# An expert kernel on one core: the path for an unguessed first expert is set ahead of the guessed one, each with its own transposition, and the last part copies fewer rows

## The chip, the cores and the metric

One core of one Trainium2 chip runs the kernel. The metric is the device time of one execution in microseconds; the kernel before has a median of 733.77 us over three executions (732.97 to 736.35). One more execution was profiled, and it took 737.84 us.

## What is computed

Three layers stand behind one another. The first is attention (4 batches, 8 heads, 576 positions, width 64; half the heads look at 32 neighbours, the other half at every 32nd position). The second is a dense layer, `h = x @ w_in`, `g = s * relu(h)**2 + b`, `x2 = g @ w_out`, over 2304 rows of 512. The third sends each row to one of eight experts:

```python
do_compute = x @ w_skip > 0
xc = x[do_compute]
e_idx = argmax(xc @ w_gate); gate_w = softmax(xc @ w_gate)[e_idx]
for e in range(8):
    mask = e_idx == e
    h = maximum(xc[mask] @ w1[e], 0)        # 512 -> 1024
    y[mask] = gate_w[mask, None] * (h @ w2[e])   # 1024 -> 512
out[do_compute] = xc + y                    # the other rows stay x
```

## The kernel before

The change lies in the third layer, in `experts()` (L1066 to L1173). The rows of one expert are taken in row tiles of 128, four tiles to a group. A group goes through these helpers:

- `gather` (L926): POOL issues four indirect DMAs (L930) that fetch four row tiles from `x2d` into `K["R"]` (the buffers `qkl` and `qks`).
- `turn` (L947): PE transposes each tile with four matmuls (L937), ACT rounds the result into `Xh` (L940), DVE puts the remainder into `Xl` (L944).
- `up` (L957): for each of eight slices of the hidden width 12 matmuls (L962) into one of two PSUM buffers `h`; ACT (L965) and DVE (L966) empty it.
- `down` (L971): for each row tile 24 matmuls (L975), one DVE instruction (L979) that scales and adds the kept row, and one indirect DMA on POOL (L980) that scatters the tile, 256 KB, to `out`.
- `keep_rows` (L1062): four ACT copies (L1064) that keep the gathered rows, since the next `gather` overwrites them.

The expert with the most rows is guessed before the last block of rows is routed. Its weights and its first 512 rows are loaded and its first `up` is done in the gaps of the last block (`fill`, L1072), all under `npre >= 512`, a count read into a register. This is the hot path. `down(3, ...)` (L1102) then does three of the four row tiles, a common `turn()` (L1119) transposes the next four tiles, and the If/Else at L1120 either does the fourth row tile, `down(4, ..., 3)` (hot), or loads and splits the weights of the expert and does its first group (general, L1122 to L1128). Behind it, the weights of the next expert are loaded into the raw buffers `wo0` to `wo7` by eight DMAs of SP (`load_raw`, L1130, issued in L904), and `groups` (L1143) does groups 1 to 3 and a last part `rest` of one to three row tiles. A loop over further experts (L1162) follows.

The order of the instructions on each engine is the order in the program, written out (`tc.manual_schedule()`); nothing of an If moves out of it. Engines wait for one another by counters: each engine counts its finished instructions, and the DMAs of POOL and of SP count in lanes, eight for each. A wait names a count, the same count whichever arm of an If ran. So the arm that runs must leave all counters where the other would have left them: on each engine an instruction that the source does not show waits until the engine's own work ahead of it is counted and then adds the other arm's share (an EVENT_SEMAPHORE record, or a larger step at the last instruction of the arm). POOL waits until the DMAs that are under way in each lane concerned have landed, and then adds to the lanes with one INC_SWDGE_SEM. An If without an Else has such an arm as well, for when it is skipped. An instruction behind an If that reads a tile which an arm may have written waits for the counts that this arm would have made, too.

In the executions told of here the hot path runs, one expert takes 18 row tiles (18 scatters in L980: four of the hot path, 14 behind it), so groups 1 to 3 run and a `rest` of two row tiles, and the loop of L1162 is skipped.

Of the kernel before, what the change touches and what calls it, by code (L numbers as in the profile page):

```python
# [191 lines left out]
def kernel(  # L192
# [70 lines left out]
    def c_v(n, fast=1, psum=0.0):  # L263
        return {"V": 0.06 + n / fast / 960 + psum}

    def c_a(n, psum=False):
        return {"A": (0.13 if psum else 0.16) + n / 1400}
# [4 lines left out]
    def c_dma(n):  # L272
        return {"SP": max(0.06, n / 300e3)}
# [300 lines left out]
    t = plan.add({"G": 0.3}, fill, 6, take=[fill_b])  # L574
# [13 lines left out]
    for n, (m, c) in enumerate(order):  # L588
# [35 lines left out]
        t = plan.add(c_dma(128 * 8 * 512), stage, prio - 2, take=[raw_b], lat=DMA)  # L624
        t = plan.add({"A": 0.58}, scale, prio, after=[t], take=[c_b], use=[raw_b])
        t = plan.add(c_v(512, 2), shift, prio, after=[t], use=[c_b])
        t = plan.add(c_v(512), sign, prio, after=[t], use=[c_b, raw_b])
        t = plan.add(c_v(512), low, prio, after=[t], use=[c_b, raw_b])
        t = plan.add({**c_a(512), **(c_v(512, 2) if c < HI_N else {})}, upper, prio, after=[t], take=[w_b], use=[c_b])
# [33 lines left out]
    t = plan.add({**c_a(512, True), **c_v(512)}, gate_row, 34, after=[gate_t], take=[gr_b], use=[gt_b])  # L663
# [253 lines left out]
    K = {}  # L917
# [21 lines left out]
    def turn_hi(pt, t):  # L939
        A.copy(K["Xh"][:, :, t * 128:(t + 1) * 128], pt[:])  # L940
# [5 lines left out]
    def turn():  # L946
        for t in range(4):  # L947
            if t < 3:
                pt = pm.tile([128, 4, 128], F32, name=("pt", "sx0", "sx1")[t])
            else:  # L950
                pt = ph.tile([128, 4, 128], F32, name="h")
            turn_in(pt, t)
            turn_hi(pt, t)
            turn_lo(pt, t)
# [13 lines left out]
    def down(nt, ids, rows, t0=0):  # L968
        for t in range(t0, nt):
            c = slice(t * 128, (t + 1) * 128)  # L970
            y = px.tile([128, DM], F32, name=f"x2p{K['ny'] % 3}")  # L971
            n = 0
            for f in range(NFE):
                for g, w in ((0, 0), (1, 0), (0, 1)):
                    PE.matmul(y[:], K["h"][f][:, g, c], W[NFE + f][:, w, :], start=n == 0, stop=n == 3 * NFE - 1)  # L975
                    n += 1
            yo = rp.tile([128, DM], F32, name="row")
            K["ny"] += 1
            V.scalar_tensor_tensor(yo[:], y[:], ids[:, t, 1:2].bitcast(F32), rows[t], op0=ALU.mult, op1=ALU.add)  # L979
            put = G.indirect_dma_start(  # L980
                out, bass.IndirectOffsetOnAxis(ap=ids[:, t, 0:1], axis=0),
                yo[:], None, bounds_check=NT - 1, oob_is_err=False,
            )
            tc.declare_no_dep(put.ins, group="rows", reason="the lists name each token once")
            tc.add_to_no_dep_group("rows", put.ins)
# [73 lines left out]
        V.tensor_copy(lg[:].rearrange("p t e -> p (t e)"), lt[:, 0:27])  # L1059
        rt[blk] = {"lg": lg}  # L1060

    def keep_rows():  # L1062
        for t in range(4):
            A.copy(K["E"][:, t, :], K["R"][t])  # L1064

    def experts():  # L1066
        K["h"] = [wp.tile([128, 2, 512], F32R, name=f"wo{8 + f}") for f in range(NFE)]
        K["E"] = wp.tile([128, 4, DM], F32, name="xb2")
        E = [K["E"][:, t, :] for t in range(4)]
        npre = reg(pre, slice(3, 4), NT)  # L1070

        def fill(n):  # L1072
            lo, hi = FILL[n], FILL[n + 1]
            if hi > lo:
                with tc.If(npre >= 512):
                    up(512, lo, hi)

        last_x2(fill)
        route_a(NBLK - 1)
        route_exp(NBLK - 1)  # L1080
        route_b(NBLK - 1)
        route_c(NBLK - 1)
        keep_rows()
        fill(3)
        rk, cn = (pm.tile([128, 512], F32, name=n_) for n_ in ("sx0", "sx1"))
        route_rank(NBLK - 1, rk)
        tally(cn)
        route_out(NBLK - 1)
        route_list(rt[NBLK - 1])
        lt = sp.tile([128, NL, 2], I32, name="s_")  # L1090
        gi = sp.tile([128, NL], I32, name="pts", bufs=1)
        SY.dma_start(lt[:, 0:NE * NTT, :].rearrange("p (e t) c -> p e t c", e=NE), lst[:].rearrange("(e p t) c -> p e t c", p=128, t=NTT))
        fill(4)
        finish_routing(cn)
        V.memset(gi[:], NT - 1)
        V.tensor_scalar(gi[:, 0:NE * NTT], lt[:, 0:NE * NTT, 0], NT - 1, None, op0=ALU.min)
        on = (mybir.EngineType.DVE,)
        eg = reg(meta, slice(0, 1), NE - 1, on)
        s0 = reg(meta, slice(19, 20), 4, on)
        gather(gi[:, bass.ds(eg * NTT + s0, 4)])  # L1100
        with tc.If(npre >= 512):
            down(3, K["ltp"], E)  # L1102
        def copied(e, t0, n):
            ids = sp.tile([128, 4, 2], I32, name="ids")
            V.tensor_copy(ids[:, 0:n, :], lt[:, bass.ds(t0, n), :])  # L1105
            return ids

        def group(e, g):
            ids = copied(e, e * NTT + 4 * g, 4)
            up(512, 0, 2)  # L1110
            keep_rows()
            gather(gi[:, bass.ds(e * NTT + 4 * g + 4, 4)])
            up(512, 2)
            turn()
            down(4, ids, E)

        word = reg(meta, slice(28, 29), (NE << 16) + 0xFFFF)
        e0, e1, T, ni = word & 7, (word >> 3) & 7, (word >> 6) & 31, word >> 16
        turn()  # L1119
        with tc.If(npre >= 512) as done:  # L1120
            down(4, K["ltp"], E, 3)
        with done.Else():  # L1122
            for n in range(8):
                load_raw(e0, n)
            for n in range(2 * NFE):
                split_w(n)
            with tc.If(T >= 4):
                group(e0, 0)  # L1128
        for n in range(8):
            load_raw(e1, n)  # L1130

        def rest(e, T, en, r):
            if r:
                ids = copied(e, e * NTT + (T & 28), r)
                up(max(256, 128 * r), 0, 2)
                keep_rows()
            gather(gi[:, bass.ds(en * NTT, 4)])
            G.drain()
            if r:
                up(max(256, 128 * r), 2)  # L1140
                down(r, ids, E)

        def groups(e, T, en):  # L1143
            with tc.If(T >= 8):
                group(e, 1)
                with tc.If(T >= 12):
                    group(e, 2)
                    with tc.If(T >= 16):
                        group(e, 3)
            with tc.If((T & 2) == 2) as two:  # L1150
                with tc.If((T & 1) == 1) as one_more:
                    rest(e, T, en, 3)
                with one_more.Else():
                    rest(e, T, en, 2)
            with two.Else():
                with tc.If((T & 1) == 1) as one_more:
                    rest(e, T, en, 1)
                with one_more.Else():
                    rest(e, T, en, 0)

        groups(e0, T, e1)
        with tc.If(ni > 1):  # L1162
            with tc.For_i(1, ni, 1) as i:
                turn()
                word = reg(meta, bass.ds(i + 20, 1), 0x7FF)
                e, en, T = word & 7, (word >> 3) & 7, word >> 6
                for n in range(2 * NFE):
                    split_w(n)
                for n in range(8):
                    load_raw(en, n)  # L1170
                with tc.If(T >= 4):
                    group(e, 0)
                groups(e, T, en)  # L1173
# [6 lines left out]
    for i, (blk, fc, begins, ends) in enumerate(SEQ):  # L1180
# [61 lines left out]
        t = plan.add(c_a(BLK, True), relu, i - 9000, after=[m1], take=[r_b], use=[h_b])  # L1242
        if i < SQ_A:
            t = plan.add(c_a(BLK), square_a, i - 9000, after=[t], use=[r_b])
            t = plan.add(c_v(BLK, 2), scale_g, i - 9000, after=[t, consts], use=[r_b])
        else:
            t = plan.add(c_v(BLK), square, i - 9000, after=[t, consts], use=[r_b])
        t = plan.add(c_a(BLK), g_hi_a if i < SQ_A else g_hi, i - 9000, after=[t], take=[gh_b], use=[r_b])
        t = plan.add(c_v(BLK), g_lo_a if i < SQ_A else g_lo, i - 9000, after=[t], take=[gl_b], use=[r_b, gh_b])
        gts[i] = t  # L1250
        if i < NS - 2:
            t = plan.add(c_pe(DM, 9, False), mm2, i + 1.2 - 3000, after=[t, mm2s[-1] if mm2s else None] + (w_done["o", fc] if blk < 2 else []),
                         take=xbuf if begins else [], use=[gh_b, gl_b, wbuf["o", fc]])
# [171 lines left out]
```

## Time and profile before

| what | us |
|---|---|
| median of three executions | 733.77 (732.97 to 736.35) |
| the profiled execution | 737.84 |
| its span, first to last instruction | 736.1 |
| `down(3)` of the hot path on PE | 542.98 to 559.34 |
| `turn()`, `down` of the fourth tile, branch to group 1 | 559.34 to 567.55 |
| groups 1 to 3 | 567.55 to 705.42 |
| `rest` of two row tiles | 705.42 to 728.70 |
| last scatter to the end | 729.77 to 736.1 |

Times on the profile's views are from the span's start. PE is TensorE's matmuls, PEld its weight loads, DVE VectorE, ACT ScalarE, POOL GpSimd, SP SyncE; a name with q (PEldq, POOLq, SPq) is the sequencer of that engine, which runs ahead of it and executes branches and semaphore instructions. A line of the timeline is: start, duration, engine, line, operation, output from input, count, and in brackets how long the engine had been idle and what released it.

### The profile page before, as it was taken

The page shows a single profiled execution, that of the slowest core. Times are in us where ns is not written, and L with a number is a line of the kernel's source. Part 1 is how long each engine was busy: PE and PEld are TensorE (multiplying, and loading weights), DVE is VectorE, ACT ScalarE, POOL GpSimd, SP SyncE. Part 2 cuts the span into 40 slices and gives each one's busy share as a digit, 9 for nine tenths or more (in the row PEclk, how much of TensorE's full clock was granted, in tenths as well). Part 3 has the DMA queues.
Part 4 walks back from the last instruction along what each step waited for, and adds up shares of the span by engine and source line. Part 5 has one row for each costly group of instructions (what it writes and reads, how often), then busy time and mean ns, then how long its engine had stood idle before and what let it go on. Part 6 is the DMA issues. An engine that isn't in the chain of part 4 may idle for free.

```text
span 736.1 us, 12323 instructions
## 1 busy us (share of the span) xinstructions
PE 720.6 (98%) x4481; PEld 619.7 (84%) x4486; DVE 418.7 (57%) x1173; ACT 290.3 (39%) x830; POOL 64.8 (9%) x79
## 2 busy tenths in 40 slices
PE   9989999999999999999999999999999999999995
PEld 6877889998888888888888988898787888888894
DVE  3679999945567887777756654754442222312221
ACT  4768866633344444544432223543311312203120
POOL 0000000000010001000200012010023212022131
PEclk9979999999999999999999999999999999999999
DMA  8856757602233313522031106320203701112021
GB/s 274 290 158 217 233 154 217 185 18 86 67 129 93 116 60 105 173 85 76 24 106 50 47 1 196 103 76 0 86 17 114 282 29 55 33 48 67 29 78 44
DMA packets 29742, 77.70 MB, mean 106 GB/s; under 512 B 5833, under 2 KB 6953, under 8 KB 29665
## 3 DMA queue, kind: packets, MB, share of 16 engines
q1 hardware_dynamic: 25585, 65.49, 27.9%
q0 software_dynamic: 3936, 11.03, 4.8%
q8 instruction: 41, 0.67, 0.4%
q14 instruction: 36, 0.29, 0.1%
q10 hardware_dynamic: 144, 0.22, 0.1%
HBM read 60.81 MB, written 15.91 MB: 104 GB/s over the span
## 4 chain that ended last, share of the span: by engine, by line
PE 73%; DMA 11%; DVE 7%; issue 5%; ACT 2%; POOL 1%; DVEq 0%; POOLq 0%; ACTq 0%
PE x2p L1235 21%; PE h L1192 21%; PE h L962 10%; PE x2p L975 8%; DMA lo<-wgt 7%; DVE junk L745 5%; DMA out<-row,ids 4%; PE sx L490 2%; PE pt L455 2%; PE sx L414 2%; PE sx L412 1%; PE h L1345 1%; DVE r L1200 1%; PE x2p L1027 1%; PE h L414 1%
## 5 line engine op out<-in xcount | busy, mean ns | idle before, releaser
L1192 PE MATMUL h<-xb,wi 128*128 128x384 f32 x1152 | 222.7, 343 | 0.0
L1192 PEld LDWEIGHTS h<-xb,wi 128*128 128x128 f32 x1152 | 204.8, 189 | 7.5 <-issue 0.7
L1235 PE MATMUL x2p<-wo,gh 128*128 128x512 f32 x564 | 195.0, 400 | 0.0
L1235 PEld LDWEIGHTS x2p<-wo,gh 128*128 128x128 f32 x564 | 105.9, 188 | 21.4 <-issue 0.3
L1235 PE MATMUL x2p<-wo,gl 128*128 128x512 f32 x282 | 111.0, 394 | 0.0
L962 PE MATMUL h<-xb,wi 128*128 128x512 f32 (+1 forms) x480 | 103.2, 374 | 1.4 <-DVE ids L1105 1.0
L962 PEld LDWEIGHTS h<-xb,wi 128*128 128x128 f32 x480 | 83.4, 188 | 19.4 <-issue 1.6
L975 PE MATMUL x2p<-wi,wo 128*128 128x512 f32 x432 | 99.4, 390 | 0.0
L975 PEld LDWEIGHTS x2p<-wi,wo 128*128 128x128 f32 x432 | 80.7, 188 | 16.6
L1204 ACT ACTIVATE gh<-r,sbc 128x384 fp32r<-128x384 f32 x91 | 56.1, 616 | 84.3 <-DVE r L1200 41.8
L1197 ACT ACTIVATE r<-h 128x384 f32<-128x384 f32 x96 | 47.0, 490 | 104.8 <-PE h L1192 64.1
L965 ACT ACTIVATE wo<-h 128x512 fp32r<-128x512 f32 (+1 forms) x40 | 22.2, 555 | 143.6 <-PE h L962 137.6
L1209 DVE SCALAR_TENSOR_TENSOR gl<-r,sbc,gh 128x384 fp32r<-128x384 f32 x91 | 56.1, 616 | 39.9 <-ACT gh L1204 39.1
L1200 DVE SCALAR_TENSOR_TENSOR r<-r,sbc 128x384 f32<-128x384 f32 x91 | 56.0, 616 | 37.6 <-ACT r L1197 36.1
L745 DVE SCALAR_TENSOR_TENSOR junk<-row,lo 128x512 int8<-128x512 f32 x81 | 55.8, 689 | 22.8 <-DMA lo<-wgt 21.6
L966 DVE SCALAR_TENSOR_TENSOR wo<-h,wo 128x512 fp32r<-128x512 f32 (+1 forms) x40 | 25.5, 638 | 76.0 <-ACT wo L965 74.9
L1235 PEld LDWEIGHTS x2p<-wo,gl 128*128 128x128 f32 x282 | 53.1, 188 | 8.4 <-DVE gl L1209 0.3
L864 POOL DMA_INDIRECT lst<-pay,ii x18 | 19.1, 1060 | 364.4 <-DVE ii L858 333.3
L979 DVE SCALAR_TENSOR_TENSOR row<-x2p,ids,xb 128x512 f32<-128x512 f32 x14 | 10.5, 751 | 61.7 <-PE x2p L975 61.7
L980 POOL DMA_INDIRECT out<-row,ids x14 | 13.9, 994 | 106.2 <-DVE row L979 92.8
L279 ACT CAST xb<-sx 128x192 fp32r<-128x192 f32 (+5 forms) x55 | 14.2, 299 | 18.5 <-PE sx L414 4.3
L497 DVE TENSOR_TENSOR xb<-sx,xb 128x192 fp32r<-128x192 f32 (+5 forms) x63 | 17.7, 302 | 4.2 <-ACT xb L279 3.4
(501 smaller groups left out, 774.4 us busy)
## 6 DMA issues: line engine op xcount, KB each, us to landing
wo<-in_w SPq DMA_DIRECT2D x16, 512.0 KB
lo<-wgt SPq DMA_DIRECT2D x27, 256.0 KB
wo<-in_w_out SPq DMA_DIRECT2D x12, 512.0 KB
x2d<-row SPq DMA_DIRECT2D x24, 256.0 KB
qks<-in_qkstr SPq DMA_DIRECT2D x6, 882.0 KB
wo<-in_w_in SPq DMA_DIRECT2D x10, 512.0 KB
out<-row SPq DMA_DIRECT2D x18, 256.0 KB
qkl<-in_qkloc SPq DMA_DIRECT2D x5, 864.0 KB
```

The lines of the kernel that those rows point to most:

```text
L414: PE.matmul(sc[0:nq, i * nk:(i + 1) * nk], qt, qk[0][:, k0:k0 + nk], start=not by_pe, stop=not by_pe or i == nt - 1)
L745: V.scalar_tensor_tensor(junk[:], d["rows"][t][:], 1.0, wd["w"][:], op0=ALU.mult, op1=ALU.mult, accum_out=d["lg"][:, t, x:x + 1])
L962: PE.matmul(p[:, 0:N], W[f][:, w, k * 128:(k + 1) * 128], x[:, k, 0:N], start=n == 0, stop=n == 11)
L965: A.activation(h[:, 0, 0:N], p[:, 0:N], AF.Relu)
L966: V.scalar_tensor_tensor(h[:, 1, 0:N], p[:, 0:N], 0.0, h[:, 0, 0:N].bitcast(F32), op0=ALU.max, op1=ALU.subtract)
L975: PE.matmul(y[:], K["h"][f][:, g, c], W[NFE + f][:, w, :], start=n == 0, stop=n == 3 * NFE - 1)
L1192: PE.matmul(p[:, 0:BLK], win_t[fc][:, w, k * 128:(k + 1) * 128], x[:, k, :], start=n == 0, stop=n == 11)
L1197: A.activation(d["r"][:], d["p"][:, 0:BLK], AF.Relu)
L1200: V.scalar_tensor_tensor(d["r"][:], d["r"][:], sbc[:, 0:1], d["r"][:], op0=ALU.mult, op1=ALU.mult)
L1204: A.activation(gh[:], d["r"][:], AF.Identity, bias=sbc[:, 1:2])
L1209: V.scalar_tensor_tensor(gl[:], d["r"][:], sbc[:, 1:2], gt[i][0][:].bitcast(F32), op0=ALU.add, op1=ALU.subtract)
L1235: PE.matmul(x2p[t][:], g[:, c], wout_t[fc][:, w, :], start=begins and n == 0, stop=ends and n == 2)
```

## The change

`turn()` is taken from its common place and stands once in each path. The Else arm becomes an If of its own, `npre < 512`, with the loads, the splits and the first group in it, and it stands ahead of the hot If. `keep_rows` gets a count, and `rest` copies as many row tiles as it has.

```diff
-    def keep_rows():
-        for t in range(4):
+    def keep_rows(n=4):
+        for t in range(n):
             A.copy(K["E"][:, t, :], K["R"][t])
...
-        turn()
-        with tc.If(npre >= 512) as done:
-            down(4, K["ltp"], E, 3)
-        with done.Else():
+        with tc.If(npre < 512):
+            turn()
             for n in range(8):
                 load_raw(e0, n)
             for n in range(2 * NFE):
                 split_w(n)
             with tc.If(T >= 4):
                 group(e0, 0)
+        with tc.If(npre >= 512):
+            turn()
+            down(4, K["ltp"], E, 3)
         for n in range(8):
             load_raw(e1, n)
...
                 up(max(256, 128 * r), 0, 2)
-                keep_rows()
+                keep_rows(r)
```

## Rows read from the trace of the kernel before

**Rows 1.** The page, part 1: busy time, share of the span, instructions of each engine
```profile
PE 720.6 (98%) x4481; PEld 619.7 (84%) x4486; DVE 418.7 (57%) x1173; ACT 290.3 (39%) x830; POOL 64.8 (9%) x79
```

**Rows 2.** The chain that ended last, 541 to 572 us: start, us, what
```profile
559.34 0.43 PE pt L937 x4
```

**Rows 3.** The timeline from the hot path's third tile to group 1, 547 to 570 us
```profile
559.44 0.75 DVE L979 SCALAR_TENSOR_TENSOR row<-x2p,s__5049,xb 128x512 f32<-128x512 f32 x1 [4.67 <-PE x2p L975]
...
560.46 0.97 POOL L980 DMA_INDIRECT out<-row,s__5049  x1 [3.06 <-DVE row L979]
...
560.84 5.71 PE L975 MATMUL x2p<-wi,wo 128*128 128x512 f32 x24
...
566.65 0.75 DVE L979 SCALAR_TENSOR_TENSOR row<-x2p,s__5049,xb 128x512 f32<-128x512 f32 x1 [3.73 <-issue]
...
567.55 2.95 SPq L904 DMA_DIRECT2D wo<-in_w  x4
567.55 2.81 PE L962 MATMUL h<-xb,wi 128*128 128x512 f32 x11 [0.99 <-DVE ids L1105]
567.68 0.97 POOL L980 DMA_INDIRECT out<-row,s__5049  x1 [6.24 <-DVE ids L1105]
```

**Rows 4.** Waits of SP's queue, 540 to 600 us: total, times, longest
```profile
SPq L904 <- DVE row L979: 18.0, 1, 18.0
```

**Rows 5.** Records of the If at L1120: count, ns min/median/max, first and last start
```profile
L1120 PEldq COMPARE_BRANCH  x2: 73/1862/3652, 558.7 to 562.3; - x2
...
L1120 POOLq INC_SWDGE_SEM  x1: 794/794/794, 567.8 to 567.8; - x1
```

**Rows 6.** The timeline, 726 to 737 us: the last matmuls and the last scatter
```profile
725.82 2.88 PE L975 MATMUL x2p<-wi,wo 128*128 128x512 f32 x12
...
729.77 1.00 POOL L980 DMA_INDIRECT out<-row,ids  x1 [4.42 <-DMA out<-row,ids]
```

**Rows 7.** Records of the If at L1162, which is skipped
```profile
L1162 POOLq EVENT_SEMAPHORE  x6: 17/30/695, 732.6 to 733.8; - x6
...
L1162 PEldq COMPARE_BRANCH  x1: 5046/5046/5046, 725.0 to 725.0; - x1
...
L1162 POOLq INC_SWDGE_SEM  x1: 226/226/226, 733.8 to 733.8; - x1
```

**Rows 8.** DMA queues, 560.4 to 563.2 us: packets, MB, share of 16 engines
```profile
q0 software_dynamic: 80, 0.26, 24.1%
```

**Rows 9.** Scatters of L980, whole run: time from issue to landing
```profile
DMA to landing us min/median/max: 2.7/2.8/3.8
```

**Rows 10.** DMA queues, 570 to 573.2 us
```profile
q1 hardware_dynamic: 216, 0.79, 72.4%
q0 software_dynamic: 80, 0.26, 20.2%
```

**Rows 11.** Stretches: us, busy PE, PEld, DVE, ACT, POOL, granted clock, DMA share, GB/s
```profile
60.00:62.00 2.00, 0.56 (x6) 0.43 (x5) 2.00 (x6) 1.40 (x8) 0.00 (x0) 1.00 0.58 221
...
734.00:736.00 2.00, 0.00 (x0) 0.00 (x0) 0.00 (x0) 0.00 (x0) 0.00 (x0) 0.50 0.02 4
36.00:38.00 2.00, 0.85 (x21) 0.72 (x22) 2.00 (x9) 1.66 (x9) 0.00 (x0) 0.91 0.85 331
...
46.00:48.00 2.00, 2.00 (x8) 2.00 (x7) 1.70 (x4) 0.00 (x0) 0.00 (x0) 0.53 0.06 6
```

**Rows 12.** The timeline, 606 to 660 us: the first matmuls of group 2
```profile
613.55 22.57 PE L962 MATMUL h<-xb,wi 128*128 128x512 f32 x96
```

**Rows 13.** The timeline of `rest`, 660 to 737 us: copies, emptying and matmuls
```profile
708.83 1.13 ACT L1064 COPY xb<-qkl 128x512 f32<-128x512 f32 x2
...
709.86 1.14 ACT L1064 COPY xb<-qks 128x512 f32<-128x512 f32 x2
...
711.79 6.02 PE L962 MATMUL h<-xb,wi 128*128 128x256 f32 x48 [0.46 <-DVE wo L966]
```

**Rows 14.** Records of the If at L1101, around `down(3)`
```profile
L1101 PEldq COMPARE_BRANCH  x2: 73/121/169, 539.1 to 555.1; - x2
```

## The prediction

> **What bounds the kernel now.** The page's busy times come first: PE is busy for 98% of the span [rows 1], so a change counts for what it adds to, or takes from, PE's idle time. The chain of waits then gives the place: the third tile of the hot path ends on PE at 559.34 us, where the first transposition of `turn()` starts at once [rows 2]. The timeline shows what follows: the fourth tile's 24 matmuls end at 560.84 + 5.71 = 566.55, and group 1 starts at 567.55 after 0.99 us of idleness [rows 3]. That gap is an arm's end: DVE's last instruction of the arm ends at 566.65 + 0.75 = 567.40, and SP, PE and POOL go on within 0.3 us of it. SP had waited 18.0 us for that one instruction before it loads the next expert's weights [rows 4], though no instruction of the hot arm touches the raw buffers. So instructions behind an If wait for counts that stand in for the other arm. The sequencer records of the If show POOL's part in it, an INC_SWDGE_SEM at 567.8 [rows 5]. I read next how long it takes at an If that is skipped, L1162: the last scatter is issued at 729.77 [rows 6], and POOL's INC_SWDGE_SEM comes at 733.8, behind a wait of 0.695 us, and takes 0.226 us [rows 7].
>
> **The change part by part.** The sums are made against the profiled execution (737.84 us: span 736.1 and 1.74 around it); the median of the runs is 4.07 us lower, and I carry the difference over to it.
>
> *A new wait ahead of the turn.* The general path, with a turn, a gather and four scatters in it, is now skipped just ahead of the hot turn. POOL must level its lanes there, and for that the three scatters of `down(3)` must have landed. The hot transposes read `K["R"]`, which the general path's gather writes, so PE waits for that levelling; in the kernel before nothing stood between. The steps: DVE ends the third tile at 559.44 + 0.75 = 560.19, POOL issues its scatter at 560.46 [rows 3]. Without company its 80 packets are gone by 563.2 [rows 8], 2.7 us after the issue, as in the median of the landings, 2.8 [rows 9]. But DVE's levelling at 560.2 also releases SP's eight weight loads, seven microseconds earlier than now. The row for that company stands in the trace: the fourth tile's scatter is issued at 567.68, just behind the first load at 567.55 [rows 3], and its 80 packets run only between 570 and 573.2, among 216 of the loads [rows 10]. That is up to 5.5 us; I take 5.4, since issue and loads have the same order and distance here (560.46, and about 560.3 for the load). Landing at 560.46 + 5.4 = 565.9, with 0.3 for POOL's waits and INC_SWDGE_SEM (0.226) [rows 7], PE restarts at 566.2 and not at 559.34: +6.9 us. The lower bound is 0, if PE need not wait for POOL; with a landing of 2.7 it is +4.1. Nothing covers it: behind the first transpose on PE stand the other 15, the 24 matmuls and group 1; ACT and DVE wait for the transposes, and POOL's next scatter for DVE.
>
> The Trainium skill (DMA: Bandwidth & Descriptors, section "Anatomy of one DMA — SWDGE (gpsimd) path") puts one such DMA at about 2.0 us plus its bytes over 436 GB/s, an estimate of 2.6 us for 256 KB. The 2.7 us without company agree, the 5.4 us beside the loads do not; by the page the sum below would be that of the rival with the short landing.
>
> *TensorE's clock.* After the last matmul, at 725.82 + 2.88 = 728.70 [rows 6], the granted clock is 0.50 in the stretch from 734 to 736, the lower of its two levels, 1.2 GHz [rows 11]: a silence of some 5 us lowers it. One of 1.4 us (0.56 busy of 2, at 60 to 62) does not. Mid-kernel the lower level lasted from 36 to 38 until the end of 46 to 48, some 10 us, over patchy work [rows 11]. A silence of 6.9 us should lower it too. Half speed costs half of the time that it lasts: 0 if it does not fall, 5 us if it lasts as long as there. Dense work follows here, so I take 4 us of it: +2.0.
>
> *The gap behind the fourth tile goes.* The hot arm is no longer levelled by its own last DVE instruction; group 1 needs DVE's part of the turn, done during the fourth tile. From group 1 to group 2, at such a boundary, PE's matmuls of L962 follow with no idle time in their row [rows 12]. -1.0 [rows 3], with 0 as the other bound.
>
> *`rest` copies two tiles instead of four.* The four copies hold ACT from 708.83 to 711.00, and PE waits 0.46 us for the emptying behind them [rows 13]. With two they end at 709.96, earlier by 1.04, more than the wait. -0.5; between 0 and -1.0.
>
> *Branches and code.* PE's branch over the Else took 3.652 us [rows 5], run by its sequencer ahead of matmuls in its queue. The jump over the general path now comes when the sequencer leaves `down(3)`, at 555.1 [rows 14], and ends at 558.8, still ahead of 559.34; the dearest jump, 5.046 [rows 7], would end at 560.2, inside the new wait. 0 as long as the wait is there, +0.9 if it is not. The second copy of the turn does not run, and the extra compares lie in the wait: 0. The earlier loads end before group 1's gather: 0, since PE does not wait for that gather now.
>
> The sum: +6.9 + 2.0 - 1.0 - 0.5 = +7.4. The profiled execution would take 745.2, the median 733.77 + 7.4 = 741.2 us.
>
> **The rivals.**
>
> *Short landing.* The scatter lands after 2.7 to 3.8 us [rows 9], because the loads' packets come too late to disturb it. For it: its descriptors are issued as early as the first load. Against it: the same order gave the late landing [rows 3, 10]. PE restarts at 563.5 to 564.6, +4.1 to +5.2, less 1.5, with 0 to 2 for the clock: 736.4 to 739.5, middle 737.9.
>
> *A long low clock.* As the first forecast, but the lower level lasts 10 us as at 36 to 48 [rows 11]: +5.0 instead of +2.0, 744.2. Against it: there matmuls were sparse.
>
> *PE does not wait for POOL* (the other side). The transposes need only counts of the gather ahead of the If, long landed, and PE, ACT and DVE level themselves in tenths of a microsecond. Then the two gains stay, -1.5, and at most the longest jump shows, +0.9: 732.3 to 733.2, middle 732.8, no change. It decides if the two paths' conditions are seen as exclusive, or if the reader of a tile waits only for the write that ran. Against it: SP's 18.0 us for an arm whose buffers it alone touches [rows 4]. The Trainium skill (Runtime: NRT & Kernel Launch, section "Instruction fetch mechanics") says that a branch to code not yet fetched holds its engine up. The 3.652 us of PE agree [rows 5]; by the page such a jump holds up the turn once nothing else does.
>
> **How the numbers follow.** The first case has 0.62, the long low clock 0.07, the short landing 0.14, no wait 0.17. With less or more low clock (0 to 3 us) and a landing up to half a microsecond off, the first case's own range is 738.7 to 742.7. For eight in ten the range must take in the long clock and most of the short landing: 736.8 to 744.5 leaves out the case without a wait. A measurement of this kernel can tell about 0.5%, 3.7 us, from no change. Slower than 737.4: 0.62 + 0.07 + 0.08 of the short landing = 0.77. Within: the rest of that, 0.06, and 0.15 of the case without a wait. Faster than 730.1 needs more than both gains: 0.02.
>
> **What would show it.** In the changed kernel's timeline PE's first transpose of the hot turn (L937) stands idle for some 7 us, POOL's INC_SWDGE_SEM of the skipped If comes just ahead of it and the third tile's landing ahead of that, and SP's loads are issued near 560, not 567. The granted clock falls near there. Group 1 follows the fourth tile without a gap; `rest` has two copies and no gap of 0.46. If the transposes start near 559.4, the first step is wrong; if they start near 563.5, the landing.

## The result and the profile after

The changed kernel takes 743.74 us (median of 6 runs, 740.84 to 747.30) beside 734.16 for the kernel before (6 runs): a ratio of 1.0131, 95% interval [1.0107, 1.0154], or +9.6 us where +7.4 was forecast. It was run once more beside the last experiment: 741.13 beside 733.01, ratio 1.0108 [1.0074, 1.0142], +8.1.

The timeline of the changed kernel around the hot turn (start, us, what, idle time before it and what ended it) answers to [rows 3]:

```profile
554.29 0.75 DVE L979 SCALAR_TENSOR_TENSOR row<-x2p,s__5049,xb 128x512 f32<-128x512 f32 x1 [4.67 <-PEq L1119]
555.27 5.90 SPq L904 DMA_DIRECT2D wo<-in_w  x8
555.32 0.97 POOL L980 DMA_INDIRECT out<-row,s__5049  x1 [3.05 <-DVEq L1119]
...
563.51 1.09 PE L937 MATMUL pt<-im,qkl 128*128 128x128 f32 x4 [9.32 <-DMA qkl<-x2d,gx]
...
566.81 6.99 PE L975 MATMUL x2p<-wi,wo 128*128 128x512 f32 x24
573.64 1.57 PE L962 MATMUL h<-xb,wi 128*128 128x512 f32 x6
```

PE stands idle for 9.32 us ahead of the first transposition, where it did not wait at all before [rows 2]. The four tiles' transpositions and the fourth tile's matmuls then take longer than they did, and group 1 (L962, at 573.64) follows without a gap. The releaser in brackets is named after the tile's last gather; that gather had landed long before, and what came last is POOL's levelling at the skipped If, line 1119. Its records (count, ns min/median/max, first and last start) answer to [rows 5]:

```profile
L1119 POOLq EVENT_SEMAPHORE  x5: 17/43/43, 555.8 to 562.4; - x5
L1119 PEldq COMPARE_BRANCH  x1: 3352/3352/3352, 550.6 to 550.6; - x1
...
L1119 POOLq INC_SWDGE_SEM  x1: 755/755/755, 562.5 to 562.5; - x1
```

POOL issues the third tile's scatter at 555.32, waits until 562.4 for it to land, and levels from 562.5 to 563.25; PE goes on 0.26 us later. PE's jump over the general path (3.35 us from 550.6) ends at 554.0, hidden. The scatter shares its time with the loads; the DMA queues from its issue to 562.2 answer to [rows 10]:

```profile
q1 hardware_dynamic: 412, 1.54, 67.5%
q0 software_dynamic: 80, 0.26, 9.4%
```

75 of its 80 packets (q0) run before 560, and the last of them between 561.5 and 562. SP's waits, which answer to [rows 4], show that the loads are let go earlier:

```profile
SPq L904 <- DVEq L1119: 10.7, 1, 10.7
```

In stretches of 2 us: the busy times of PE, PEld, DVE, ACT and POOL, and then the granted clock (third figure from the end), the DMA share and GB/s; as [rows 11]:

```profile
556.00:558.00 2.00, 0.00 (x0) 0.00 (x0) 0.00 (x0) 0.00 (x0) 0.29 (x1) 1.00 0.69 162
558.00:560.00 2.00, 0.00 (x0) 0.00 (x0) 0.00 (x0) 0.00 (x0) 0.00 (x0) 0.82 0.86 307
560.00:562.00 2.00, 0.00 (x0) 0.00 (x0) 0.00 (x0) 0.00 (x0) 0.00 (x0) 0.50 1.00 391
...
566.00:568.00 2.00, 2.00 (x9) 1.81 (x8) 1.53 (x3) 1.29 (x3) 0.00 (x0) 0.50 1.03 416
568.00:570.00 2.00, 2.00 (x8) 1.53 (x7) 0.55 (x1) 0.00 (x0) 0.00 (x0) 0.62 0.39 160
570.00:572.00 2.00, 2.00 (x10) 1.67 (x9) 0.00 (x0) 0.00 (x0) 0.00 (x0) 1.00 0.02 8
```

It falls to 0.50 (the lower level, 1.2 GHz) during PE's silence and is back at 1.00 only during the fourth tile: the 0.62 from 568 to 570 puts that near 569.5, an estimate, so PE works at the lower level for some 6.0 us. Last, the timeline of `rest`, as [rows 13]:

```profile
711.44 11.72 PE L962 MATMUL h<-xb,wi 128*128 128x256 f32 x96
...
714.85 1.13 ACT L1064 COPY xb<-qkl 128x512 f32<-128x512 f32 x2
...
723.00 11.07 PE L975 MATMUL x2p<-wi,wo 128*128 128x512 f32 x48
```

The line of the kernel before that answers to the last of these:

```profile
717.64 11.05 PE L975 MATMUL x2p<-wi,wo 128*128 128x512 f32 x48
```

Two copies, no wait on PE: from 711.44 to 723.00 are 11.56 us, where the same part took 717.64 - 705.42 = 12.22 before.

To keep the account I measure from the start of DVE's scaling of the third tile (L979) to the start of the first transposition (A), and from there to group 1's first matmul (B). In the timeline of the kernel before the first transposition is this line (the chain of [rows 2] counts it from the end of the matmul ahead of it, 559.34):

```profile
559.18 0.60 PE L937 MATMUL pt<-im,qkl 128*128 128x128 f32 x4
```

Before: A = -0.26 (559.18 against 559.44), B = 8.37 (to 567.55), in it the gap. After: A = 9.22, B = 10.13. Later runs show B without gap and at the full clock as 7.21. So the change costs 9.48 in A, 2.92 for the clock in B, and gives 1.16 (the gap) and 0.66 (`rest`) back: +10.6 us.

The two profiled spans differ by only 741.0 - 736.1 = 4.9 us, because the execution profiled before had a stretch at the lower clock from 36 to 48 us [rows 11] that this one lacks; the third tile's scaling comes at 554.29 here and at 559.44 there. Of the fourteen profiles five have such a stretch (before, e2_hot_first, e4_seven_dmas, e6_busy_pe, e9_busy30). The spread of the times goes with the clock, too: of the 24 executions of the kernel before that stand beside e7_late_put, the six above 736 us have a mean granted clock of 0.990 or 0.991, the others (731.5 to 733.8) 0.993 to 0.999. This is why what follows reads the trace in place beside the medians.

### The profile page after: what moved, and what is told of

Its sections match the earlier page's. It is cut to its first block, busy times and chain, and to the rows that moved or that the text cites. A ratio compares the mean times of both kernels' runs of the same rounds, so it can differ in the third digit from the quotient of the medians.

```text
span 741.0 us, 12346 instructions
## 1 busy us (share of the span) xinstructions
PE 718.6 (97%) x4485; PEld 618.6 (83%) x4486; DVE 418.6 (56%) x1173; ACT 290.1 (39%) x828; POOL 64.7 (9%) x79
## 4 chain that ended last, share of the span: by engine, by line
PE 86%; DMA 6%; issue 4%; ACT 1%; DVE 1%; POOL 1%; DVEq 0%; POOLq 0%; ACTq 0%
PE h L1193 28%; PE x2p L1236 27%; PE h L962 10%; PE x2p L975 7%; DMA out<-row,ids 4%; DMA qkl<-x2d,gx 3%; PE sx L490 2%; PE pt L455 2%; PE sx L412 2%; PE sx L414 2%; PE h L1346 1%; PE x2p L1027 1%; PE sx L483 1%; PE h L414 1%; PE pt L937 1%
## 5 line engine op out<-in xcount | busy, mean ns | idle before, releaser
L962 PE MATMUL h<-xb,wi 128*128 128x512 f32 (+1 forms) x480 | 103.0, 373 | 0.0
L962 PEld LDWEIGHTS h<-xb,wi 128*128 128x128 f32 x480 | 83.5, 188 | 17.5 <-issue 0.2
L979 DVE SCALAR_TENSOR_TENSOR row<-x2p,ids,xb 128x512 f32<-128x512 f32 x14 | 10.5, 751 | 61.8 <-PE x2p L975 61.8
L980 POOL DMA_INDIRECT out<-row,ids x14 | 13.9, 995 | 105.8 <-DVE row L979 92.5
```

The lines of the kernel that those rows point to most:

```text
L962: PE.matmul(p[:, 0:N], W[f][:, w, k * 128:(k + 1) * 128], x[:, k, 0:N], start=n == 0, stop=n == 11)
```

## The experiments

All were timed beside the kernel before on the same chip, and the ratio is to that; the series were run on several chips. A and B as above, us; the column of the scatter's issue to INC_SWDGE_SEM is filled where the skipped path stands ahead of the hot turn or of the fourth tile:

| run | A | B | A + B | scatter's issue to INC_SWDGE_SEM | median | before | ratio |
|---|---|---|---|---|---|---|---|
| before | -0.26 | 8.37 | 8.11 | | | | |
| changed | 9.22 | 10.13 | 19.35 | 7.2 | 743.74 | 734.16 | 1.0131 [1.0107, 1.0154] |
| e1_rest_only | -0.25 | 8.36 | 8.11 | | 732.73 | 733.72 | 0.9998 [0.9976, 1.0019] |
| e2_hot_first | -0.25 | 8.37 | 8.12 | | 733.75 | 733.72 | 1.0002 [0.9982, 1.0023] |
| e3_no_gather | 0.94 | 7.25 | 8.19 | 0.8 | 734.29 | 733.72 | 1.0009 [0.9986, 1.0031] |
| e4_seven_dmas | 2.84 | 8.87 | 11.71 | 0.9 | 735.62 | 733.72 | 1.0019 [0.9999, 1.0039] |
| e5_no_loads | 5.26 | 9.51 | 14.77 | 3.3 | 739.32 | 733.33 | 1.0079 [1.0049, 1.0109] |
| e6_busy_pe | 9.79 | 7.20 | 16.99 | 5.6 | 743.98 | 733.33 | 1.0127 [1.0093, 1.0161] |
| e7_late_put | -0.26 | 8.41 | 8.15 | | 732.01 | 733.33 | 0.9990 [0.9966, 1.0015] |
| e8_shared_turn | -0.26 | 9.50 | 9.24 | 3.1 | 734.67 | 733.33 | 1.0018 [0.9993, 1.0042] |
| e9_busy30 | 8.22 | 7.21 | 15.43 | 5.6 | 743.70 | 735.41 | 1.0102 [1.0071, 1.0133] |
| e10_skip_pe | -0.26 | 8.37 | 8.11 | | 735.05 | 735.41 | 0.9990 [0.9968, 1.0012] |
| e11_after_again | 7.39 | 8.90 | 16.29 | 5.4 | 741.13 | 733.01 | 1.0108 [1.0074, 1.0142] |
| e12_busy30_again | 8.06 | 7.22 | 15.28 | 5.5 | 740.71 | 733.01 | 1.0093 [1.0066, 1.0120] |

My theory: the hot turn waits for POOL, because a skipped path that gathers into the row tiles stands ahead of it, and POOL waits there for the third tile's scatter; the loads make that scatter late, and the silence lowers the clock. The main rival: PE is held by the jump over the longer general path.

**The small part alone.** The kernel before with `keep_rows(r)` in `rest`.

> The kernel before with one part of the change alone: rest copies only the row tiles that are left. Theory: the emptying of PSUM behind the copies comes earlier and PE's 0.46 us of waiting goes, so 0.4 to 0.7 us less than the kernel before. Rival: the time won is given back further on in the last part, no difference at all.

In the trace `rest` takes 11.52 us (700.46 to 711.98) and not 12.22, as in the changed kernel. In time 0.7 us of 733 is below what the runs can tell.

**The order.** The two Ifs change places:

```diff
+        with tc.If(npre >= 512):
+            turn()
+            down(4, K["ltp"], E, 3)
         with tc.If(npre < 512):
             turn()
...
-        with tc.If(npre >= 512):
-            turn()
-            down(4, K["ltp"], E, 3)
```

> The changed kernel with its two Ifs in the other order: the hot path with its turn first, the general path (skipped) behind it. Theory (the hot turn waits because a skipped path that gathers into the row tiles stands ahead of it): the 9.3 us of idleness on PE go, the clock does not fall, and group 1 waits about 1 us for the last levelling on DVE as in the kernel before: 733 to 734.5 us. Rival (the general path now holds a turn more, and it is the jump over it that holds PE up): 3 to 5 us stay, 737 to 739.

The whole loss is gone. Its timeline:

```profile
556.00 0.60 PE L937 MATMUL pt<-im,qkl 128*128 128x128 f32 x4
...
557.66 5.71 PE L975 MATMUL x2p<-wi,wo 128*128 128x512 f32 x24
564.37 10.98 PE L962 MATMUL h<-xb,wi 128*128 128x512 f32 x46 [0.99 <-DVEq L1122]
```

The turn starts at once, and the gap of 0.99 is back ahead of group 1. The general path with its own turn is there as in the changed kernel, so its length is not what costs; its place is.

**The gather.** The changed kernel, and the general path's first group leaves out its gather; that path does not run with these inputs.

```diff
-        def group(e, g):
+        def group(e, g, ga=True):
...
-            gather(gi[:, bass.ds(e * NTT + 4 * g + 4, 4)])
+            if ga:
+                gather(gi[:, bass.ds(e * NTT + 4 * g + 4, 4)])
...
-                group(e0, 0)
+                group(e0, 0, ga=False)
```

> The changed kernel; the general path's first group leaves out its gather (that path is skipped with these inputs). Order, turns, branches and scatters stay. Theory (PE waits for POOL's levelling only because the skipped path writes the row tiles by a gather): the transposes start within 1 us of the third tile's end, the clock stays, 732 to 734 us. Rival (any skipped path with DMAs of POOL in it, or the branch itself, holds PE up): 741 to 744 as the changed kernel.

```profile
555.85 0.63 PE L937 MATMUL pt<-im,qkl 128*128 128x128 f32 x4 [1.03 <-DVEq L1120]
```
```profile
L1120 PEldq COMPARE_BRANCH  x1: 4061/4061/4061, 551.2 to 551.2; - x1
...
L1120 DVEq EVENT_SEMAPHORE  x1: 21/21/21, 555.7 to 555.7; - x1
...
L1120 POOLq INC_SWDGE_SEM  x1: 772/772/772, 556.7 to 556.7; - x1
```

Nothing but an instruction that never runs was taken out, and 8.3 of the 9.3 us of idleness go. POOL still levels, at 556.7, but PE no longer waits for it: it goes on at 555.85, earlier than that. What stays is 1.03. PE's jump took 4.06 us, to 555.3, some 0.4 past the end of the third tile's matmuls (554.8), and DVE's levelling at 555.7, behind its scaling of the third tile, comes last; the line names it. So the prediction's 0.9 for a jump that no wait covers is near the 1.03 by luck: the jump itself is 0.4 of it. The time is a little above the expected 732 to 734, the ratio no change.

**The landing.** The general path's first group writes 3 of its 4 row tiles, so that the skipped path holds 7 DMAs of POOL. They take 8 semaphores in turn, so that the one on which the third tile's scatter lands has nothing to be levelled.

```diff
-        def group(e, g):
+        def group(e, g, n=4):
...
-            down(4, ids, E)
+            down(n, ids, E)
...
-                group(e0, 0)
+                group(e0, 0, 3)
```

> The changed kernel; the general path's first group writes 3 of its 4 row tiles, so that the skipped path holds 7 of POOL's DMAs and not 8, and the one semaphore on which the third tile's scatter lands has nothing to be levelled (that path is skipped with these inputs). Theory (the wait is mostly for that landing): PE still waits for POOL, which issues the scatter (0.97 us) and levels (0.76 us), but not for the landing: some 3.9 us of idleness instead of 9.3, 735 to 738.5 us. Rival (the wait is for POOL's levelling as such, or the branch): 741 to 744.

```profile
557.99 0.97 POOL L980 DMA_INDIRECT out<-row,s__5049  x1 [3.04 <-DVEq L1119]
559.81 0.63 PE L937 MATMUL pt<-im,qkl 128*128 128x128 f32 x4 [2.94 <-DMA qkl<-x2d,gx]
```
```profile
L1119 POOLq INC_SWDGE_SEM  x1: 774/774/774, 558.9 to 558.9; - x1
```

POOL levels 0.9 us after the issue, not 7.2, and PE's idleness is 2.94 us. The theory holds: the rest of the 9.3 was the landing. Yet the clock fell after the silence of 2.94 us, which I had not expected; B is 8.87, 1.66 above 7.21. PE was back at work from 559.81 on, and by the 0.75 from 560 to 562 the fall came near 561, an estimate, more than 1 us later:

```profile
560.00:562.00 2.00, 2.00 (x16) 2.00 (x15) 0.86 (x2) 1.48 (x3) 0.00 (x0) 0.75 0.84 244
562.00:564.00 2.00, 2.00 (x7) 1.62 (x6) 1.72 (x3) 0.75 (x2) 0.00 (x0) 0.50 1.01 383
564.00:566.00 2.00, 2.00 (x10) 1.61 (x9) 0.00 (x0) 0.00 (x0) 0.00 (x0) 0.90 1.03 410
```

**The company of the loads.** The changed kernel without the loads of a next expert's weights, which are left out.

```diff
-        for n in range(8):
-            load_raw(e1, n)
```

> The changed kernel without the eight loads of the next expert's weights behind the hot path (left out; with these inputs only one expert has tokens left, so nothing reads them). Theory (the scatter lands late because the loads run beside it): the landing falls from 6.8 us to about 2.7, PE's idleness ahead of the turn from 9.3 to 5.2 or 5.6 us, the clock still falls: 738.5 to 740.5 us. Rival (the landing takes this long by itself): 743 to 744.

```profile
561.08 1.08 PE L937 MATMUL pt<-im,qkl 128*128 128x128 f32 x4 [5.35 <-DMA qkl<-x2d,gx]
```
```profile
DMA to landing us min/median/max: 2.9/2.9/2.9
```

The landing takes 2.9 us and the idleness 5.35, in the range expected; 739.32 us. The loads are the rest of the wait, 4.0 us of the first profile's and 2.1 of the second's.

**The clock.** The changed kernel with matmuls ahead of the hot turn whose sums nobody reads; first 36 in one buffer, then 30 in two.

```diff
         with tc.If(npre >= 512):
+            pad = ph.tile([128, 512], F32, name="h")
+            for n in range(36):
+                PE.matmul(pad[:], W[0][:, 0, 0:128], K["Xh"][:, 0, :], start=True, stop=True)
             turn()
```

> The changed kernel with 36 matmuls of 128x512 (their sums read by nobody) ahead of the hot turn, in its If, so that PE works for 8.2 of the 9.3 us in which it waits. Theory (3.1 us of the loss are the clock, which falls because PE is silent): the turn takes 1.75 us and the fourth tile 5.5 at the full clock, the wait itself stays, 740 to 741.5 us. Rival (the clock is not what the turn and the fourth tile lose): 743 to 745.

> The changed kernel with 30 matmuls of 128x512 (their sums read by nobody) ahead of the hot turn, in two PSUM buffers, so that the order of the buffers behind it is that of the changed kernel. They fill 6.9 of the 9.3 us of PE's wait and end before the landing is known, unlike the 36 of the earlier run, which ended after it, and they shift no buffer. Theory (3.1 us of the loss are the clock): the granted clock stays at 1.00, from the third tile's end to group 1 it takes 16.0 to 16.6 us and not 19.5, and the time is 740.5 to 741.5 us. Rival (the clock is no cost here, the loss is the wait alone): 19 us there, 743 to 745.

> The changed kernel with the 30 filling matmuls, once more, beside the changed kernel on the same chip. Theory (the fallen clock costs 3.1 us; the filling gives 1.0 back ahead of the last part's matmuls, as in its first profile): 1.5 to 3.5 us less than the changed kernel beside it. Rival (the clock costs nothing in the end): no difference to it.

In all three the granted clock stays at 1.00 and B is 7.20 to 7.22. Of e9_busy30:

```profile
562.00:564.00 2.00, 1.65 (x7) 1.41 (x8) 0.00 (x0) 0.00 (x0) 0.97 (x1) 1.00 0.41 86
564.00:566.00 2.00, 2.00 (x10) 1.58 (x10) 0.00 (x0) 0.00 (x0) 0.00 (x0) 1.00 0.82 256
566.00:568.00 2.00, 2.00 (x10) 1.63 (x9) 0.00 (x0) 0.00 (x0) 0.00 (x0) 1.00 0.84 256
568.00:570.00 2.00, 2.00 (x13) 1.64 (x12) 0.00 (x0) 0.00 (x0) 0.00 (x0) 1.00 1.00 305
```

So the 2.92 us in B are the clock, shown in place. In time they do not show: 743.98, 743.70 and 740.71, the first two in the range of the rival (743 to 745). The last stands beside the changed kernel on its chip (741.13): 0.4 less, not the 1.5 to 3.5 expected. The filling outlasts the wait there (A is 8.06 against 7.39), and each of the three has a new gap ahead of the last part's matmuls, which I had put down to the odd buffer and which two buffers did not take away:

```profile
710.68 11.76 PE L962 MATMUL h<-xb,wi 128*128 128x256 f32 x96 [0.72 <-PE x2p L975]
```

Of the 1.68 that B gains (7.22 for 8.90), 0.67 in A and 0.72 there go back, which leaves 0.3. The traces show what stands in that gap: PE's jump at the If ahead of the last part, `(T & 1) == 1`, took 3.72 us from 706.7 to 710.4 in e12_busy30_again (3.82 in e6_busy_pe, 3.80 in e9_busy30), past the end of group 3's matmuls at 710.0. In the eleven other profiles the same jump took 0.28 to 0.40 us. So the added matmuls made another jump longer; why is open.

**Where the gap of 0.99 goes.** Three runs look for a version without wait and without gap. The first takes the fourth tile's scaling and scatter out of the hot path into a third If behind the general path; the second has one turn ahead of both Ifs; the third adds a skipped If of matmuls alone ahead of group 2.

```diff
         with tc.If(npre >= 512):
             turn()
-            down(4, K["ltp"], E, 3)
+            y3 = down_mm(3)
...
                 group(e0, 0)
+        with tc.If(npre >= 512):
+            put_out(y3, 3, K["ltp"], E)
```

> The order of the run with the hot path first, and the scaling, adding and scattering of the fourth tile in a third If, behind the general path. Theory: DVE levels the skipped general path while the fourth tile's matmuls run, group 1 has nothing to wait for, and the 0.99 us ahead of it go: 1.0 to 1.6 us less than the kernel before, 732 to 733. Rival (PE's jump of 3.35 us over the general path, or the third If, is late next): 733.5 to 735.

> The changed kernel's two Ifs in their order, but with one turn ahead of both, as in the kernel before. Theory (only the transposes read what the skipped path's gather writes): the turn starts at the third tile's end; the fourth tile then waits some 1 to 1.5 us for DVE's levelling behind the turn, and group 1 follows it without a gap: 733 to 735 us. Rival (the wait for the landing moves to the fourth tile): 738 to 741.

> The run with the hot path first, and ahead of group 2 one more If that is skipped and holds matmuls alone, no DMA, no work of DVE or ACT. Theory (an If that is skipped with work of PE in it lets PE's queue run empty, which makes the gap of 0.99 us that stands wherever such an If stands): a gap of 0.5 to 1.1 us ahead of group 2's first matmul, where there is none now, and 0.5 to 1.1 us more in all, about 734.5. Rival (the gap ahead of group 1 is the wait for DVE's last instruction of the hot path): no gap ahead of group 2, 733.7.

The row that decides, of e7_late_put, e8_shared_turn and e10_skip_pe in this order:

```profile
562.00 22.63 PE L963 MATMUL h<-xb,wi 128*128 128x512 f32 x96 [1.03 <-DVE ids L1112]
```
```profile
558.58 5.72 PE L975 MATMUL x2p<-wi,wo 128*128 128x512 f32 x24 [2.03 <-DVEq L1120]
```
```profile
610.27 22.64 PE L962 MATMUL h<-xb,wi 128*128 128x512 f32 x96 [0.30 <-PEq L1148]
```

With the late put a gap of 1.03 stands where 0.99 stood; its 732.01 lies in the range expected, but not by the mechanism, and the ratio is no change. What holds PE there is open: its jump (3.35 us from 557.0) was over at 560.4, but its levelling came at 561.0, behind the fourth tile's matmuls, and only then did DVE scale that tile; the trace names DVE's copy of `ids` behind that. With the shared turn the landing costs nothing, but the fourth tile waits 2.03 us for DVE's levelling behind the turn, more than the 1 to 1.5 expected. The skipped If of matmuls alone costs 0.30, less than my theory's 0.5 and more than the rival's nothing. PE's jump there took only 0.23 us, so 0.30 is what PE's own queue costs with a short jump; in the other places the trace names DVE as the last to let PE go on.

**Once more.** The changed kernel, on the chip of e12_busy30_again.

> The changed kernel once more, beside the next one on the same chip. Theory: as in its first profile, PE idles 8 to 9.5 us ahead of the hot turn, with a landing of the third tile's scatter of 5 to 7 us, and it takes 9 to 11 us more than the kernel before. If the landing of 6.8 us of the first profile was an outlier, it is 5.0 to 5.5 here, and the idleness 7.5 to 8 us.

```profile
554.57 0.97 POOL L980 DMA_INDIRECT out<-row,s__5049  x1 [3.06 <-DVEq L1119]
560.94 1.09 PE L937 MATMUL pt<-im,qkl 128*128 128x128 f32 x4 [7.48 <-DMA qkl<-x2d,gx]
```
```profile
L1119 POOLq INC_SWDGE_SEM  x1: 759/759/759, 560.0 to 560.0; - x1
```

The levelling comes 5.4 us after the issue, where it was 7.2 in the first profile, and the idleness is 7.48 us. The sum in place is +7.65 in A, +1.69 for the clock, -1.16 and -0.66: +7.5, with +8.1 in the medians.

## Why the prediction held, and where its terms were off

The sum gave +7.4, and the two series show +9.6 and +8.1. The first median, 743.74, lies above the first case's own range (738.7 to 742.7) and inside the whole range (736.8 to 744.5) only because that was widened for the long low clock (744.2), while the excess came mostly from the wait (9.5 for 6.9): that part is luck. The second, 741.13, lies in both.

*The new wait* (forecast +6.9; +9.5 and +7.7 in the two profiles). The mechanism is shown: the wait needs the skipped path ahead of the turn (e2_hot_first) and a gather in it that writes what the transposes read (e3_no_gather), and its length needs a DMA in it on the semaphore of the scatter in flight (e4_seven_dmas) and the loads beside that scatter (e5_no_loads). Its size has two errors. The landing beside the loads was taken as 5.4 from one row; the two profiles show 7.2 and 5.4 from issue to levelling, and the three runs with filling matmuls 5.5 and 5.6, so 5.4 was near the usual value and the first profile's 7.2 stands alone. What made it so long is open. The step between landing and PE was taken as 0.3, with an INC_SWDGE_SEM of 0.226 from another If [rows 7], though the record of this very place stood in [rows 5] with 0.794; it took 0.755 and 0.759, and PE went on 0.9 to 1.0 us after its start. From issue to PE's restart the forecast had 5.7 us; it took 8.2 and 6.4.

*Short landing* (forecast 0.14; 737.9). Ruled out with the loads there, and e5_no_loads makes the case: the landing is 2.9 us, but the time 739.32, since the late step and the clock stay. The Trainium skill (DMA: Bandwidth & Descriptors, section "Anatomy of one DMA — SWDGE (gpsimd) path"), by which the estimate was 2.6 us, agrees with the 2.9 alone and not with the landing beside the loads.

*The clock* (forecast +2.0; +2.9 and +1.7). Right in kind, and its size between the two measured values: PE worked at the lower level for some 6.0 and 3.5 us (by the stretches of the two profiles), where the forecast took 4. The silence of some 5 us that the forecast read from [rows 11] is no lower bound: in e4_seven_dmas the clock fell after 2.94 us, in e3_no_gather it stayed at 1.00 after 1.03. The rival of the long low clock (forecast 0.07, +5.0) did not come.

*The gap behind the fourth tile* (forecast -1.0; -1.16 with the overlap of two matmul groups). Right here, but not a gain for the taking: wherever the skipped If stands and no longer wait covers it, 1 to 2 us of levelling show (0.99 ahead of group 1, 1.03 ahead of the turn, 2.03 ahead of the fourth tile). The changed kernel hides it in the larger wait.

*`rest`* (forecast -0.5; -0.66) was right. *Branches* (forecast 0; 0) was right for the changed kernel; the +0.9 without the wait is near the 1.03 of e3_no_gather by luck, since the jump itself is 0.4 of that and DVE's levelling ends it. *PE does not wait for POOL* (forecast 0.17) is refuted by the 9.32 and 7.48; e3_no_gather, which makes that case, stands at 734.29.

No version here beats the kernel before by what the runs can tell: the best median is e7_late_put's, 732.01 at a ratio of 0.9990 [0.9966, 1.0015].

## What to carry to other kernels

A branch that never runs still has to be accounted for by the engines that would have worked in it, and whoever reads behind it what it might have written waits for that; so put the path that runs ahead of the one that is skipped, and look what DMAs are in flight where a path with DMAs is skipped. Price such a step by the records of the place itself, not by those of another If, and let a landing beside other transfers have a range, not a value. A gain of a gap at one If is worth little until it is seen where that levelling shows next.

## What the hardware showed that was not expected

PE's jump over a skipped path took 0.23 us (16 matmuls alone, e10_skip_pe), 0.36 (the general path without its last row tile, e4_seven_dmas), 3.35 (the whole general path, the changed kernel) and 4.26 (the same program in its second profile). The jump at one and the same If of the last part took 0.28 to 0.40 us in eleven programs and profiles and 3.72 to 3.82 in the three with filling matmuls ahead of it; what decides is open. POOL's INC_SWDGE_SEM took 0.755 to 0.779 us for skipped paths of 4, 7 or 8 DMAs alike, against 0.226 at the If of [rows 7]. And the granted clock fell to 0.50 after 2.94 us of silence on PE between dense stretches, and more than 1 us after PE was at work again.
